# A fused S5 scan and gated MLP: the residual stored early and the gated product added to it by accumulating DMA, with a new order of the work

## The chip, the cores and the metric

The kernel runs on one core of one Trainium2 chip. Its engines, as the profile names them, are TensorE (PE, with its weight loads as PEld), VectorE (DVE), ScalarE (ACT), GpSimd (POOL) and SyncE (SP), which here only issues DMAs. The metric is device time of one execution in microseconds, as the median of several runs. A profiled execution also gives a trace: its span runs from the first to the last instruction and is a little shorter than the execution's time.

## The reference

The input `x` has 2048 tokens of 448 channels, in bfloat16. It is normalized twice: once as the input of both branches, and once more inside branch B.

```python
def _A_ref(x, Lambda_re, Lambda_im, B_re, B_im, C_re, C_im, log_dt, Dskip):
    dt = jnp.exp(log_dt)
    Lam_bar = jnp.exp(dt * Lam)
    B_bar = ((Lam_bar - 1.0) / Lam)[:, None] * Bmat
    Bu = jnp.einsum("bld,pd->blp", x + 0j, B_bar)
    for t in range(L):
        h = Lam_bar[None, :] * h + Bu[:, t, :]
    y = 2.0 * jnp.einsum("blp,dp->bld", hseq, Cmat).real + x * Dskip[None, None, :]

def _B_ref(x, w1, b1, w2, b2):
    y = _layernorm(x, axis=-1)
    h = _gelu(jnp.einsum("bsd,df->bsf", y, w1) + b1)
    return jnp.einsum("bsf,fd->bsd", h, w2) + b2

xn = _layernorm(x, axis=-1)
s = _A_ref(xn, A_Lambda_re, ...)
g = _silu(_B_ref(xn, B_w1, B_b1, B_w2, B_b2))
return x + s * g
```

Branch A is a complex diagonal recurrence over all 2048 tokens with 448 states. Branch B is an MLP with 1792 hidden units. The output is the residual `x` plus the product of both.

## The kernel before

The tokens are worked in four groups of 512. A group has two blocks (`b`), and a block two tiles of 128 tokens (`r`), so there are eight blocks and sixteen tiles. The 448 channels or states lie as three tiles of 128 and one of 64 on the partitions. For each group the kernel does the following.

- **Normalization.** `ln_stats` takes mean and variance of each tile of `x_all`: groups 0 and 1 on VectorE (BATCH_NORM_STATS2 and AGGREGATE, L441 and L445; L457 and L458 for the first group), groups 2 and 3 on ScalarE in two passes with an accumulator (L433 and L434, the groups in `SUMS`). `ln_scale` turns them into scales by a power on GpSimd or by two Newton steps on VectorE. `ln_apply` writes the normalized tiles `xn_sb` (for branch A) and `xn2_sb` (for branch B, both norms in one; the profile leaves numbers in names out and shows `xn_sb` for both), L514 on VectorE or L515 on ScalarE. `xt` transposes them by DMA into `xnT` and `xn2T`. The first group goes through `first_norm`: tile by tile, its scale by Ln and Exp on ScalarE or by a power on GpSimd (L462), and its transposes by TensorE, copied out of PSUM by L471 or L472.
- **Branch A.** `bu` multiplies `xnT` by the B matrices into `u_sb` (TensorE L665, and L685 for the last tile; copies out of PSUM at L682, L683, L687, L688). `ssm` rotates `u_sb` by cosine and sine tables (`WT`), so that a real scan with a decay is left (L709, seven scans of 512 tokens), and rotates the result back into `h_sb`. These rotations are the wide products of VectorE (L701 to L703 and L729 to L731, 128x3072). The end of a group's scan is turned into the start value `cur` of the next by four small GpSimd operations (L722 to L725), the carry.
- **Branch B.** `mm1` is the first layer of the MLP in seven pairs of hidden tiles (TensorE L665, Gelu on ScalarE L746). In the first group the pairs below `HALF` are done block by block, with matmuls of 256 columns (`mm1_half`, L758). `mm2` is the second layer (L779: 14 matmuls for each tile, 56 for a group), and Silu on ScalarE gives the gate `g_sb` (L782).
- **Output.** `ym` multiplies `h_sb` by the C matrices and `xnT` by the diagonal of `Dskip` (L796 and L799), VectorE multiplies by the gate into `t3` (L802, `t` in the profile), adds `x` for a whole block (L815, into `o_sb`, which the profile calls `tmp`), and SP stores it to `out`. The last block goes tile by tile, its last tile in two parts (L806).

The matmuls that keep TensorE busy before its first real work multiply `still` by itself (I0 to I9, L825).

All of this is written as tasks with what they read and write. The order is a table, `ORDER`, one list for all engines: each engine gets its tasks in that order and waits at each one for what the task depends on. `SECOND` says which tasks run on their second engine, and `BANKS` which of the eight PSUM banks each tile of results takes; a bank's next user waits until its last has been read. So an engine that waits holds up all that stands behind it on its queue. DMAs stand in the queue of the engine that issues them.

Of the kernel before, what the change touches and what calls it, by code (L numbers as in the profile page):

```python
# [10 lines left out]
F32 = dt.float32  # L11
# [36 lines left out]
class Plan:  # L48
# [50 lines left out]
    def dma(self, eng, out_ap, in_ap, reads=(), writes=(), prio=0.0, nbytes=0, transpose=False, dur=0.45):  # L99
        sem = f"d{self.ndma}"  # L100
        self.ndma += 1
        self._sem(sem)

        def fn(e):
            if transpose:
                return e.dma_start_transpose(out_ap, in_ap)
            return e.dma_start(out_ap, in_ap)  # L107
# [97 lines left out]
ST I2 11 I7 20 12 18 17 19 I1 75 76 0 1 13 16 15 2 3 14 80 81 22 23 I0 I3 21 5 9 I8 4 82 PV 77 24 25 27 36 26 78 6 7 T0 83 T2 I6 79 I4 I9 85  # L205
86 87 90 91 38 96 8 84 H010 92 88 34 93 H000 40 I5 T3 T1 95 144 41 46 97 89 101 118 94 42 43 45 10 H04 32 117 33 H001 39 98 102 109 115 110
H02 48 44 55 122 H011 105 116 223 119 49 56 47 103 106 H03 50 104 99 121 227 123 35 29 107 H05 28 100 H06 108 57 DH 51 54 53 61 111 311 222
224 228 124 125 112 120 138 225 128 229 193 113 312 129 126 58 64 313 114 59 60 62 65 66 67 226 206 207 198 194 230 231 232 31 30 145 238
202 314 127 130 235 69 199 131 132 135 203 137 233 208 209 133 136 234 396 200 195 204 241 196 166 240 315 205 201 397 197 U01 167 U00 U02
162 164 160 236 139 H13 242 134 237 163 141 63 165 317 316 239 169 H11 282 319 H10 68 283 161 170 320 168 318 171 172 173 174 180 398 H14  # L210
278 279 276 284 142 37 285 U10 H15 243 H12 181 70 74 286 280 179 176 277 52 143 177 175 U12 244 399 73 400 287 281 71 H16 247 72 183 288 178
140 248 289 146 148 149 147 150 151 182 189 321 H20 154 155 186 152 U11 187 361 290 153 184 245 246 323 156 158 185 291 293 188 295 402 362
401 403 249 157 190 191 192 297 159 405 218 254 253 219 404 294 216 406 325 322 298 210 292 250 212 296 326 217 255 211 H26 251 H35 H23 373
213 259 374 367 368 H21 454 327 252 261 363 324 262 263 258 260 455 U20 U22 H34 364 U21 328 265 256 257 329 330 332 452 220 H22 333 264 272
266 268 267 271 331 H24 273 274 275 339 338 340 453 365 369 370 269 H30 H33 444 450 307 308 214 445 270 334 343 411 299 305 300 366 335 410
451 221 345 301 H36 H25 412 H32 302 306 346 344 407 408 409 456 336 348 448 215 457 371 347 U30 U32 413 337 341 417 372 H31 449 342 418 414
349 U31 350 375 446 415 309 354 351 353 310 352 355 416 382 447 383 357 356 358 359 360 424 380 423 376 458 425 432 431 378 379 377 392 386
419 459 420 429 384 428 433 421 430 435 393 422 426 465 427 303 434 440 381 436 463 437 460 304 439 441 438 442 443 387 385 461 390 467 388
389 391 394 462 464 469 395 468 473 470 471 472 477 474 475 476 466 478 479 480 481 482 483 484
""".split()]  # L220
SECOND = [int(k) if k.isdigit() else k for k in """
77 79 84 87 94 115 130 150 161 167 183 187 230 270 316 317 319 320 322 323 325 326 355 407 408 410 411 418
""".split()]
BANKS = [int(k) if k.isdigit() else k for k in """
3 3 0 0 1 5 1 3 3 2 5 3 0 6 5 0 4 2 2 0 6 6 0 2 0 2 4 5 6 7 4 5 4 6 1 2 6 0 4 0 4 2 0 6 0 2 6 6 4 7 5 6 1 0 1 2 6 0 7 2 6 2 2 0 6 0 2 3 4 5
3 2 6 1 0 0 2 3 6 6 4 4 4 4 2 6 0 5 7 4 5 6 5 4
# [12 lines left out]
def bass_recurrent_scan__ssm_conv_s5__mixer_channel_mlp__prompt_kernel(  # L239
# [14 lines left out]
    NB, NG, NF, NK, HALF = 8, 4, 14, 512, 2  # L254
    PK, SUMS = 3, (2, 3)
# [3 lines left out]
    with ExitStack() as es:  # L259
# [6 lines left out]
        eps = SB("eps", [128, 1], F32)  # L266
# [24 lines left out]
        junk = SB("junk", [128, D])  # L291
# [19 lines left out]
        t3 = SB("t3", [128, 2, 2, D])  # L311
# [24 lines left out]
        with nc.Block():  # L336
# [13 lines left out]
            preload("natural_log_exp_and_others", [], "logs", "exp")  # L350
            pool(lambda e: e.memset(eps[:], LN_EPS * LN_EPS), [], ["eps"], 0.1)
# [75 lines left out]
            def ln_stats(g, blocks=(0, 1)):  # L427
                if g in SUMS:
                    for b in blocks:
                        for r in range(2):  # L430
                            q = r * 2 + b
                            src, mv = x_all[:, xa(2 * g + b, r), :], lnmv[:, g % 2, q, :]
                            act([lambda e, src=src, mv=mv: e.activation(junk[:], src, ACT.Identity, scale=-1.0 / D, accum_out=mv[:, 0:1]),  # L433
                                 lambda e, src=src, mv=mv: e.activation(junk[:], src, ACT.Square, bias=mv[:, 0:1], accum_out=mv[:, 1:2])],  # L434
                                [f"x{2 * g + b}"], [f"mv{g % 2}_{q}", "junk"], 1.3)
                            kb.tasks[-1].chain = True
                    return
# [44 lines left out]
            def ln_scale(g, blocks=(0, 1)):  # L482
# [14 lines left out]
                if sign < 0:  # L497
                    power.append(lambda e: e.tensor_scalar(w(3), w(3), -1.0, None, op0=ALU.mult))
# [399 lines left out]
```

## Time and profile before

| | |
|---|---|
| time, median of three runs | 149.23 us (149.13 to 149.49) |
| profiled execution | 149.4 us |
| its span | 147.7 us |
| TensorE busy | 141.8 us, 96% |
| VectorE busy | 128.1 us, 87% |
| ScalarE busy | 106.3 us, 72% |
| GpSimd busy | 46.0 us, 31% |
| granted TensorE clock | 1.000 |

Busy time is an average over a start, a long full middle and a tail, and these have different limits. So the chain of work that ended last, and the waits of the engines on it, say more than the shares. A row of a group gives the line, the engine, the operation, output and inputs, shapes and count; then the busy time, the mean of one in ns, and the idle time before them with what ended it. In a timeline row the first two numbers are start and length in us.

### The profile page before, as it was taken

Reading aid. Unit: us, or ns where it says so; the run is one execution under the profiler, and the core shown is the slowest. Engines: PE = TensorE matmul, PEld = TensorE weight load, DVE = VectorE, ACT = ScalarE, POOL = GpSimd, SP = SyncE. Lnnn points to the kernel's source line nnn. Section 1 sums busy time; section 2 is a strip of 40 time slices with the busy share of each in tenths; the row PEclk is TensorE's granted clock in tenths of the full one; section 3 lists DMA queues with packets and bytes.
Section 4 is the critical chain, followed back from the end, with each engine's and each line's share of the span. In section 5 each row is a group of like instructions: output and inputs, shape, how many; then the busy total and the mean of one; then the engine's idle time right before and its main releaser. Section 6 shows DMA issues by size and latency. Waiting matters only on the chain.

```text
span 147.7 us, 2854 instructions
## 1 busy us (share of the span) xinstructions
PE 141.8 (96%) x1078; PEld 74.6 (51%) x1078; DVE 128.1 (87%) x168; ACT 106.3 (72%) x173; POOL 46.0 (31%) x89
## 2 busy tenths in 40 slices
PE   6979999998999999999998999999999999999992
PEld 2557744543555545555553454555435455555562
DVE  1846999806599999999999998999999999999994
ACT  2469899899999999999939997962999112291300
POOL 2488788930009592800000003900009300000000
DMA  4989999998859101007080002019003000103033
GB/s 103 286 249 388 274 307 150 198 95 157 158 127 96 28 18 22 0 0 142 18 157 8 0 18 80 4 22 204 16 7 98 0 0 0 40 0 98 0 127 124
DMA packets 32084, 14.09 MB, mean 95 GB/s; under 512 B 24131, under 2 KB 31686, under 8 KB 32070
## 3 DMA queue, kind: packets, MB, share of 16 engines
q1 hardware_dynamic: 31376, 13.83, 42.7%
q8 instruction: 8, 0.13, 0.4%
q10 hardware_dynamic: 694, 0.07, 0.4%
q14 instruction: 6, 0.05, 0.1%
HBM read 5.63 MB, written 1.84 MB: 51 GB/s over the span
## 4 chain that ended last, share of the span: by engine, by line
PE 86%; DMA 6%; DVE 4%; SPq 2%; issue 1%; ACT 0%; ACTq 0%; DVEq 0%
PE psum L665 37%; PE psum L779 29%; PE psum L796 14%; DMA xnT<-xn_sb 3%; DMA x_all<-in_A_x_dram 3%; PE psum L685 2%; PE psum L799 2%; SPq L107 2%; DVE t L802 1%; PE psum L771 1%; DVE lnst L457 1%; DVE xn_sb L514 1%; DVE WT L621 0%; PE psum L469 0%; DVE tmp L806 0%
## 5 line engine op out<-in xcount | busy, mean ns | idle before, releaser
L665 PE MATMUL psum<-xn2T,w_sb 64*128 64x512 bf16 (+1 forms) x420 | 45.2, 362 | 0.9 <-ACT cw L547 0.9
L779 PE MATMUL psum<-w_sb,gT 128*128 128x448 bf16 x224 | 43.7, 353 | 0.1
L746 ACT ACTIVATE gT<-psum,b1f 128x512 bf16<-128x512 f32 x52 | 32.1, 688 | 8.0 <-PE psum L665 7.8
L665 PEld LDWEIGHTS psum<-xn2T,w_sb 64*128 64x128 bf16 x420 | 24.4, 108 | 18.9 <-ACT cw L547 1.0
L779 PEld LDWEIGHTS psum<-w_sb,gT 128*128 128x128 bf16 x224 | 21.5, 98 | 21.6 <-issue 1.5
L709 DVE TENSOR_TENSOR_SCAN s_f<-cw,cur,v_sb 128x512 f32<-128x512 f32 x21 | 25.5, 1266 | 0.0
L796 PE MATMUL psum<-CQ,h_sb 128*128 128x448 bf16 (+2 forms) x119 | 24.8, 342 | 0.0
L665 PE MATMUL psum<-xnT,BT 64*128 64x512 bf16 x168 | 20.4, 376 | 1.0 <-DVE xn_sb L514 0.6
L722 POOL TENSOR_TENSOR cwk<-s_f,ang 128x8 f32<-128x8 f32 x3 | 3.5, 1166 | 45.5 <-ACT s_f L719 45.5
L782 ACT ACTIVATE g_sb<-psum 128x448 bf16<-128x448 f32 x16 | 8.1, 536 | 10.7 <-PE psum L779 10.6
L796 PEld LDWEIGHTS psum<-CQ,h_sb 128*128 128x128 bf16 x119 | 10.9, 98 | 7.5 <-issue 0.4
L665 PEld LDWEIGHTS psum<-xnT,BT 64*128 64x128 bf16 x168 | 8.3, 94 | 11.0 <-PE psum L665 1.2
L713 ACT ACTIVATE s_b<-s_f 128x3072 bf16<-128x3072 f32 x4 | 11.1, 2774 | 2.9 <-DVE s_f L709 2.8
L682 ACT ACTIVATE u_sb<-psum 128x1024 bf16<-128x1024 f32 x10 | 10.1, 1019 | 0.4 <-PE psum L665 0.3
L515 ACT ACTIVATE xn_sb<-x_all,lnw 128x512 bf16<-128x512 bf16 x13 | 10.1, 810 | 0.0
L802 DVE TENSOR_TENSOR t<-psum,g_sb 128x448 bf16<-128x448 f32 (+2 forms) x17 | 9.7, 587 | 0.3 <-PE psum L796 0.2
L709 DVE TENSOR_TENSOR_SCAN s_f<-cw,v_sb 128x512 f32<-128x512 f32 x7 | 8.1, 1208 | 0.0
L601 POOL TENSOR_TENSOR DG<-ident,Dbc 128x128 bf16<-128x128 bf16 (+1 forms) x4 | 3.6, 917 | 13.3 <-DMA Dbc<-in_A_Dskip_dram 13.3
L825 PE MATMUL psum<-still 128*128 128x128 bf16 (+1 forms) x30 | 6.4, 364 | 1.2 <-DVE still L339 1.0
L730 DVE TENSOR_TENSOR pb<-s_b,WT 128x3072 bf16<-128x3072 bf16 x4 | 7.0, 1752 | 0.4 <-ACT s_b L713 0.3
L703 DVE TENSOR_TENSOR v_sb<-pa,pb 128x3072 bf16<-128x3072 bf16 x4 | 7.0, 1756 | 0.1
L731 DVE TENSOR_TENSOR h_sb<-pa,pb 128x3072 bf16<-128x3072 bf16 x4 | 7.0, 1755 | 0.1
(123 smaller groups left out, 175.2 us busy)
## 6 DMA issues: line engine op xcount, KB each, us to landing
out_dram<-tmp SPq DMA_DIRECT2D x7, 224.0 KB, 2.3
w_sb<-in_B_w_dram SPq DMA_DIRECT2D x6, 256.0 KB, 5.2
x_all<-in_A_x_dram SPq DMA_DIRECT2D x3, 448.0 KB, 6.8
w_sb<-in_B_w_dram SPq DMA_DIRECT2D x3, 448.0 KB, 7.5
u_sb<-u_sb SPq DMA_DIRECT2D x8, 64.0 KB, 2.1
s_b<-s_b SPq DMA_DIRECT2D x8, 64.0 KB, 1.9
w_sb<-in_B_w_dram SPq DMA_DIRECT2D x2, 128.0 KB, 3.1
x_all<-in_A_x_dram SPq DMA_DIRECT2D x2, 112.0 KB, 2.5
```

The source lines that it names most:

```text
L515: ("act", lambda e: e.activation(dst, src, ACT.Identity, bias=nb, scale=rs), 0.81)]
L665: return lambda e: e.matmul(out(k), wt(k, d, halves[h]), rhs(k, d, halves[h]), start=first and d == 0, stop=not first and d == 3)
L682: kb.either(("act", lambda e: e.activation(u_sb[:, i, :, :], psum[:, bank.b:bank.b + 2, :], ACT.Copy), 1.02), ("dve", lambda e: e.tensor_c ...
L703: dve(lambda e: e.tensor_tensor(v_sb[:, 0:3, :, :], pa[:], pb[:], ALU.add), ["pa", "pb"], ["v"], 1.76)
L709: dve(lambda e, i=i, ri=ri, init=init: e.tensor_tensor_scan(s_f[:, i, ri, :], col(R1, i).to_broadcast([128, NK]), v_sb[:, i, ri, :], init, ...
L713: act(lambda e: e.activation(s_b[:, 0:3, :, :], s_f[:, 0:3, :, :], ACT.Copy), SF, ["sb"], 2.76)
L730: dve(lambda e: e.tensor_tensor(pb[:], wide(s_b, 1), WT[:, 0:3, 1:3, :], ALU.mult), ["sb"] + WK, ["pb"], 1.76)
L746: act([lambda e, k=k: e.activation(gT[:, gb, 2 * j + k, :], psum[:, bank.b + k, :], ACT.Gelu_apprx_tanh, bias=b1f[:, 2 * j + k:2 * j + k + ...
L779: fns = [lambda e, fi=fi, bk=bk, q=q: e.matmul(psum[:, bk.b, 0:D], gT[:, gb, fi, q * 128:(q + 1) * 128], w2_sb[:, fi, :], start=False, sto ...
L782: act(lambda e, gs=gs, bk=bk: e.activation(g_sb[:, gs, :], psum[:, bk.b, 0:D], ACT.Silu), [bk.key] + (["silu"] if g == 0 else []), [f"g{gs ...
L796: fns = [lambda e, k=k: e.matmul(psum[:, bank.b, c0:c1], h_sb[:, hb, k, k0:k0 + 128], CQ[:, k, c0:c1], start=(k == 0), stop=(k == 6)) for ...
L802: dve(lambda e: e.tensor_tensor(t3[:, ob, r, c0:c1], psum[:, bank.b, c0:c1], g_sb[:, gs, c0:c1], ALU.mult), [bank.key, f"g{gs}"], [f"t3{ob ...
```

## The change

- Seven of the eight blocks of `x` are stored to `out` by SP as soon as they are loaded. Where VectorE added `x` to a block's gated product and SP stored the sum (L815), GpSimd now issues a DMA that adds `t3` to what lies in `out`. It waits for the block's two gate multiplies and for the early store. `t3` has four buffers instead of two. The last block is done as before.
- The statistics of all groups are taken on VectorE; `SUMS` and the ScalarE passes are gone.
- The first group's scales all come from a power on GpSimd; the multiply and add before it stands on VectorE. Ln and Exp, their table and `eps` are gone, and ScalarE loads the Gelu table at once.
- `HALF` is 3 instead of 2: one more pair of hidden tiles of the first group is done block by block.
- `ORDER`, `SECOND` and `BANKS` are new. Among what moves: the first block's second load of `x` (`x1`) stands ahead of the first weights on SP, one 128x2048 Abs of the tables goes to ScalarE, five normalizations go from VectorE to ScalarE, and on GpSimd the first of the accumulating DMAs stands between the first and the second carry, the next between the second and the third, and five behind the third.

```diff
@@ dma
+            if accum:
+                return e.dma_start(out_ap, in_ap, accum_op=ALU.add)
@@ tables of the order
-ST I2 11 I7 20 12 18 17 19 I1 75 76 0 1 13 16 15 2 3 14 80 81 22 23 I0 I3 21 5 9 I8 4 82 PV 77 24 25 27 36 26 78 6 7 T0 83 T2 I6 79 I4 I9 85
+ST I0 11 17 12 13 18 I3 9 16 4 20 0 I1 14 15 22 21 19 24 23 I7 10 I2 1 74 75 79 80 76 77 84 81 82 T0 85 86 89 I5 T2 90 8 I6 I8 87 91 78 I4
...
-    NB, NG, NF, NK, HALF = 8, 4, 14, 512, 2
-    PK, SUMS = 3, (2, 3)
+    NB, NG, NF, NK, HALF = 8, 4, 14, 512, 3
+    PK = 3
-        t3 = SB("t3", [128, 2, 2, D])
+        t3 = SB("t3", [128, 4, 2, D])
-            preload("natural_log_exp_and_others", [], "logs", "exp")
+            preload("gelu_apprx_tanh_and_others", [], "warm", "gelu")
@@ ln_stats
-                if g in SUMS:
-                    for b in blocks:
...
-                            act([lambda e, src=src, mv=mv: e.activation(junk[:], src, ACT.Identity, scale=-1.0 / D, accum_out=mv[:, 0:1]),
-                                 lambda e, src=src, mv=mv: e.activation(junk[:], src, ACT.Square, bias=mv[:, 0:1], accum_out=mv[:, 1:2])],
...
@@ first_norm
-                        dve(lambda e, q=q: e.bn_aggr(lnmv[:, 0, q, :], lnst[:, q, :]), [f"st{q}"], [f"mv0_{q}"], 0.18)
-                        t = kb.either(("act", [lambda e, var=var, r1=r1: e.activation(r1, var, ACT.Ln, scale=1.0 + LN_EPS, bias=eps[:]),
-                                               lambda e, r1=r1: e.activation(r1, r1, ACT.Exp, scale=-0.5)], 0.53),
...
+                        kb.add("dve", [lambda e, q=q: e.bn_aggr(lnmv[:, 0, q, :], lnst[:, q, :]),
+                                       lambda e, var=var, w0=w0: e.tensor_scalar(w0, var, 1.0 + LN_EPS, LN_EPS * LN_EPS, op0=ALU.mult, op1=ALU.add)],
+                               [f"st{q}"], [f"mv0_{q}", f"w0{q}"], dur=0.3, chain=True)
+                        pool(lambda e, w0=w0, r1=r1: e.tensor_tensor(r1, w0, mhalf[:, 0, :], ALU.pow), [f"w0{q}", "mhalf"], [f"r1{q}"], 0.57)
...
@@ ym
-                gs, ob = n % 8, b
+                gs, ob = n % 8, (2 * g + b) % 4
...
                 if r and not last:
-                    t = xa(2 * g + b, 0)
-                    o2r = o_sb[:, ob, :].rearrange("p (r d) -> p r d", r=2)
-                    dve(lambda e: e.tensor_tensor(o2r, t3[:, ob, :, :], x_all[:, t:t + 3:2, :], ALU.add), [f"t3{ob}_0_0", f"t3{ob}_1_0"] + xk(2 * g + b),
-                        [f"o{ob}_0_0", f"o{ob}_1_0", f"o{ob}_1_256"], 0.64)
-                    kb.dma("sp", dram_ap(out, off, [[D, 128], [256 * D, 2], [1, D]]), o2r,
-                           reads=[f"o{ob}_0_0", f"o{ob}_1_0", f"o{ob}_1_256"], writes=[f"out{g}{b}"], nbytes=229376)
+                    kb.dma("pool", dram_ap(out, off, [[D, 128], [256 * D, 2], [1, D]]), t3[:, ob, :, :],
+                           reads=[f"t3{ob}_0_0", f"t3{ob}_1_0", f"out{g}{b}"], writes=[f"sum{g}{b}"], nbytes=229376, dur=1.2, accum=True)
@@ main
+            for k in range(2 * NG - 1):
+                t = xa(k, 0)
+                kb.dma("sp", dram_ap(out, xrow(k), [[D, 128], [256 * D, 2], [1, D]]), x_all[:, t:t + 3:2, :],
+                       reads=xk(k), writes=[f"out{k // 2}{k % 2}"], nbytes=229376)
```

The tables move instructions on every engine. Three places show it, with the lines of the kernel that the rows belong to (the changed kernel's line numbers are 11 to 18 lower). The first is VectorE at the start, in `first_norm`. Before:

```order
L457 BN_STATS lnst<-x_all 128x6
L458 BN_AGGR lnmv<-lnst 128x2
L457 BN_STATS lnst<-x_all 128x6
L458 BN_AGGR lnmv<-lnst 128x2
L465 TENSOR_SCALAR xn_sb<-x_all,lnmv,lnw 128x512 x2
L457 BN_STATS lnst<-x_all 128x6
L458 BN_AGGR lnmv<-lnst 128x2
L457 BN_STATS lnst<-x_all 128x6
```

With the change, where L448 is the small scale before the power:

```order
L446 BN_STATS lnst<-x_all 128x6
L447 BN_AGGR lnmv<-lnst 128x2
L448 TENSOR_SCALAR lnw<-lnmv 128x1
L446 BN_STATS lnst<-x_all 128x6
L447 BN_AGGR lnmv<-lnst 128x2
L448 TENSOR_SCALAR lnw<-lnmv 128x1
L451 TENSOR_SCALAR xn_sb<-x_all,lnmv,lnw 128x512
L446 BN_STATS lnst<-x_all 128x6
L451 TENSOR_SCALAR xn_sb<-x_all,lnmv,lnw 128x512
```

Each tile has one instruction more, and the third tile's statistics stand between the normalizations of the first two. The second place is ScalarE between the first group's last Gelu and the first copies of `u_sb`. Before:

```order
L348 ACT_TABLE_LOAD
L619 ACTIVATE WT<-s_f 128x4x512
L782 ACTIVATE g_sb<-psum 128x448
L620 ACTIVATE WT<-s_f,sgn 128x4x512
L433 ACTIVATE junk,lnmv<-x_all 128x448
L434 ACTIVATE junk,lnmv<-x_all,lnmv 128x448
L782 ACTIVATE g_sb<-psum 128x448 x2
L433 ACTIVATE junk,lnmv<-x_all 128x448
L434 ACTIVATE junk,lnmv<-x_all,lnmv 128x448
L782 ACTIVATE g_sb<-psum 128x448
L682 ACTIVATE u_sb<-psum 128x1024 x2
```

With the change:

```order
L498 ACTIVATE xn_sb<-x_all,lnw 128x512 x2
L553 ACTIVATE ang<-ang 128x16
L348 ACT_TABLE_LOAD
L602 ACTIVATE WT<-s_f 128x4x512
L598 ACTIVATE s_f<-s_f 128x4x512
L603 ACTIVATE WT<-s_f,sgn 128x4x512
L498 ACTIVATE xn_sb<-x_all,lnw 128x512 x2
L765 ACTIVATE g_sb<-psum 128x448 x3
L498 ACTIVATE xn_sb<-x_all,lnw 128x512
L665 ACTIVATE u_sb<-psum 128x1024 x2
L765 ACTIVATE g_sb<-psum 128x448
L665 ACTIVATE u_sb<-psum 128x1024
```

The statistics are gone, an Abs over the table (L598) and normalizations (L498) have come, and no Silu stands between the two Sin. The third place is TensorE behind the first group's output tiles. Before (L665 with `xnT` is `bu`, with `xn2T` it is `mm1`):

```order
L799 MATMUL psum<-DG,xnT 128x128
L796 MATMUL psum<-CQ,h_sb 128x448 x6
L665 MATMUL psum<-xn2T,w_sb 128x512 x56
L665 MATMUL psum<-xnT,BT 128x512 x16
L665 MATMUL psum<-xn2T,w_sb 128x512 x8
L665 MATMUL psum<-xnT,BT 128x512 x26
```

With the change (L762 is `mm2`):

```order
L782 MATMUL psum<-DG,xnT 128x128
L779 MATMUL psum<-CQ,h_sb 128x448 x6
L762 MATMUL psum<-w_sb,gT 128x448 x28
L668 MATMUL psum<-xnT,BT 128x512 x4
L648 MATMUL psum<-xnT,BT 128x512 x36
```

Half of the second group's `mm2` has come behind the output tiles, and the third group's `mm1` pairs that stood there now stand ahead of them.

More of the change, by code (lines that the diff above doesn't have):

```diff
@@ L209 @@
[L209 to L216, printed above, removed]
@@ L479, in first_norm @@
                                 lambda e: e.tensor_tensor(n0, mean, r0, ALU.mult), lambda e: e.tensor_scalar(n0, n0, -1.0, None, op0=ALU.mult)],
-                       [f"mv0_{q}" for q in range(4)] + ["mhalf"], ["lnw0_0", "lnw0_1"], dur=1.2, chain=True)
+                       [f"mv0_{q}" for q in range(4)] + ["mhalf"], ["lnw0_0", "lnw0_1"], dur=1.6, chain=True)
             def ln_scale(g, blocks=(0, 1)):
```

56 lines of the change are left out of this document (24 added, 32 removed).

## The prediction

> **What bounds the kernel now.** I read the page first: the busy times, then the chain that ended last.
>
> ```profile
> span 147.7 us, 2854 instructions
> PE 141.8 (96%) x1078; PEld 74.6 (51%) x1078; DVE 128.1 (87%) x168; ACT 106.3 (72%) x173; POOL 46.0 (31%) x89
> PE 86%; DMA 6%; DVE 4%; SPq 2%; issue 1%; ACT 0%; ACTq 0%; DVEq 0%
> ```
>
> TensorE is busy in 96% of the span and makes 86% of the chain. The change takes none of its real work away, so time can come only from before its first real matmul, from its holes, and from what follows its last one. The second view is busy time by stage (columns: stretch, its length, busy us of PE, PEld, DVE, ACT, POOL, granted clock, DMA share, GB/s).
>
> ```profile
> 40.00:80.00 40.00, 39.57 (x308) 20.56 (x304) 39.31 (x40) 37.11 (x59) 12.92 (x14) 1.00 0.35 60
> 80.00:120.00 40.00, 40.00 (x316) 19.62 (x313) 38.68 (x37) 29.54 (x41) 10.54 (x8) 1.00 0.17 41
> 120.00:140.00 20.00, 20.00 (x122) 10.77 (x120) 19.70 (x20) 7.25 (x10) 0.00 (x0) 1.00 0.10 25
> ```
>
> From 40 us on VectorE is as full as TensorE (39.31 and 38.68 of 40), and until 80 ScalarE nearly so (37.11). The clock is 1.00 throughout. Three engines are close to setting the end at once, so relief of one is worth little unless the others follow. Third, the chain in order of time (start, us, what):
>
> ```profile
> 8.88 1.07 PE psum L665 x16
> 10.96 9.35 PE psum L665 x104
> 21.37 1.26 PE psum L779 x6
> 22.68 9.63 PE psum L779 x50
> 35.56 18.95 PE psum L665 x174
> 75.08 4.68 DMA xnT<-xn_sb
> ```
>
> And the waits of TensorE behind its holes (us in total, times, longest):
>
> ```profile
> PE psum L665 <- DVE xn_sb L514: 0.6, 1, 0.6
> PE psum L665 <- DMA xnT<-xn_sb: 0.4, 1, 0.4
> ```
>
> Real matmuls start at 8.88, run on without a pause from 10.96, and have holes of 0.6 (before 35.56) and 0.4 (at 79.8, behind the transpose begun at 75.08). Last, the end, by the timeline:
>
> ```profile
> 138.06 0.43 DVE L733 TENSOR_TENSOR h_sb<-pa 128x512 bf16<-128x512 bf16 x1
> 138.91 0.36 PE L799 MATMUL psum<-DG,xnT 128*128 128x128 bf16 x4
> 144.33 0.66 PE L796 MATMUL psum<-CQ,h_sb 128*128 128x192 bf16 x6
> 145.50 0.26 DVE L806 TENSOR_TENSOR tmp<-t,x_all 128x192 bf16<-128x192 bf16 x1
> ```
>
> TensorE ends at 144.33+0.66 = 144.99, and 2.7 us follow (gate, add, last store). The last group's four output tiles need `h_sb`, which VectorE finishes at 138.49; the first of them begins about 0.2 before its diagonal matmuls of 138.91. So VectorE leads by only some 0.2 us there.
>
> **The change part by part.** The sum is made against the profiled execution: 149.4 us, the span of 147.7 and 1.7 around it. It lies 0.17 above the median of the three runs, 149.23.
>
> ```profile
> L815 DVE TENSOR_TENSOR tmp<-t,x_all 128x896 bf16<-128x896 bf16 x7 | 4.3, 618 | 0.3 <-DMA out_dram<-tmp 0.2
> L441 DVE BATCH_NORM_STATS2 lnst<-x_all 128x6 f32<-128x448 bf16 x4 | 2.4, 617 | 0.0
> L445 DVE BATCH_NORM_AGGREGATE lnmv<-lnst 128x2 f32<-128x6 f32 x4 | 0.7, 168 | 0.0
> L683 DVE CAST u_sb<-psum 128x1024 bf16<-128x1024 f32 x2 | 2.5, 1225 | 2.8 <-PE psum L665 2.8
> L434 ACT ACTIVATE junk<-x_all,lnmv 128x448 bf16<-128x448 bf16 x8 | 5.3, 668 | 0.3
> ```
>
> *VectorE.* The residual adds go: 7 x 0.618 = 4.3 us. The statistics of groups 2 and 3 come from ScalarE, 8 x 0.617 + 8 x 0.168 = 6.3; all eight BATCH_NORM_STATS2 lie ahead of the first wide product, beside TensorE's first group, where VectorE has room. In the full stage, from the first wide product (39.83 before) to the last group's `h_sb`, I count: 4 adds fewer (-2.5; the other three stood behind `h_sb`), one gate multiply moved behind it (-0.6), 4 aggregates (+0.7), one CAST of `u_sb` more (+1.2), and one scaling of `tmp`, one small cast and one DG tile (+1.0, estimated from operations of that size). That is -0.2 of some 98 us: in this stage the relief is spent again. The last `h_sb` then follows the first wide product, which waits for ScalarE (holes, below), and comes at 137.5 to 138.7; TensorE will want it at about 138.1. I charge 0.1, bounds 0 and 0.6.
>
> *ScalarE* loses the two passes per tile of its statistics (the second alone is 5.3 us) and gains five normalizations and an Abs over 2048 columns; the gain is cover in the stage where it is nearly full.
>
> *Start.* `x1` is loaded ahead of the first weights; all first scales come from POOL; VectorE has one more small instruction per tile and takes the second tile's statistics before it normalizes the first.
>
> ```profile
> 3.40 0.63 DVE L457 BATCH_NORM_STATS2 lnst<-x_all 128x6 f32<-128x448 bf16 x1 [2.41 <-DMA x_all<-in_A_x_dram]
> 4.67 0.56 POOL L462 TENSOR_TENSOR lnw<-lnw,mhalf 128x1 f32<-128x1 f32 x1
> 6.72 1.09 ACT L472 ACTIVATE xn2T<-psum 128x512 bf16<-128x512 bf16 x2 [1.13 <-PE psum L469]
> 8.48 0.16 ACT L547 ACTIVATE cw<-psum 128x12 f32<-128x12 f32 x1
> ```
>
> From 3.40 two tiles of statistics, aggregate and small scale (about 1.0 each, the power of 0.56 beside them), the first normalization, the third tile's statistics and the second normalization end at about 6.95. Transposes and the second ScalarE copy (half of 1.09) end at 8.0. Before, 8.88 was set by the parameter copy that ends at 8.64; now that copy stands behind. So the first real matmul comes at 8.0, and the fourth tile's transposes end at about 9.75 (before: 10.96). In between only 8 matmuls of 256 columns fit (before: 16 by 9.95). What is left behind 9.75 is 76 half and 56 full matmuls: HALF 3 splits one more pair. A full one is 18.95/174 = 0.109, a half one 1.07/16 = 0.067: 5.1+6.1 = 11.2 with 0.3 for the bias; by the same prices 70 full and 40 half were 10.6 before, measured 10.41. The first group ends at 9.75+11.3 = 21.1 instead of 21.37: -0.2, bounds -0.6 and +0.4.
>
> *Old holes.* The 0.6 was a wait for a normalization on VectorE; it is replaced by the bank waits below (-0.6). At the 0.4, two of group 1's four output tiles of the MLP (28 matmuls, 28 x (1.26+9.63)/56 = 5.4 us) now stand between the tile that frees `xnT` and the matmuls that read it; the transpose takes 4.7. So -0.4, with 0.7 us of cover; without that cover the full 4.7 would show.
>
> *New holes.* At 20 to 40 us ScalarE does what VectorE did, and TensorE's next banks wait for it.
>
> ```profile
> L348 ACT ACT_TABLE_LOAD x3 | 3.8, 1283 | 2.9 <-issue 2.8
> L619 ACT ACTIVATE WT<-s_f 128x2048 bf16<-128x2048 f32 x1 | 1.9, 1910 | 0.4 <-ACT L348 0.4
> L515 ACT ACTIVATE xn_sb<-x_all,lnw 128x512 bf16<-128x512 bf16 x13 | 10.1, 810 | 0.0
> L682 ACT ACTIVATE u_sb<-psum 128x1024 bf16<-128x1024 f32 x10 | 10.1, 1019 | 0.4 <-PE psum L665 0.3
> L782 ACT ACTIVATE g_sb<-psum 128x448 bf16<-128x448 f32 x16 | 8.1, 536 | 10.7 <-PE psum L779 10.6
> ```
>
> A run of Gelu from the timeline shows how such operations follow each other:
>
> ```profile
> 49.33 2.40 ACT L746 ACTIVATE gT<-psum,b1f 128x512 bf16<-128x512 f32 x4
> ```
>
> From 21.1: two Gelu pairs (2.3), two normalizations (1.6), a small Abs, the table load and the 0.4 behind it (1.9), three operations over 2048 columns (5.8), two normalizations (1.6), three Silu (1.6): 14.8, which frees the bank of the third `bu` tile at 35.9; a normalization, two copies, a Silu and a copy more (4.3) bring the third `u_sb`, and with it VectorE's first wide product, to 40.2. Operations in a row overlap (four Gelu in 2.40, where four times the single one is 2.75), so 34.9 and 39.0 are as likely. TensorE reaches the third `bu` tile at 21.1 + 10.9 (MLP) + 28 x 0.109 = 35.1, and the next group's first bank, freed by the second copy, at 37.6, against 37.6 to 38.6. Holes here: 0 to 1.0. From 55 to 70 the Gelu pairs again free TensorE's banks at about the time that it wants them: 0 to 0.4 more. I take 0.5, nearer the overlapped end.
>
> *Stores and accumulating DMAs.* Seven stores of `x` leave the SP queue between the transposes of the first two groups and later.
>
> ```profile
> 88.27 0.52 SPq L107 DMA_DIRECT2D out_dram<-tmp  x1
> ```
>
> Each holds the transposes behind it up by one such issue (0.52). At the first group the transposes leave at about 24 and 26 and are wanted at 32.0, when the MLP ends: 4.7 to landing leaves over 1 us, so 0; with that cover gone each store costs its 0.5. The tail's last add and store stay as they are.
>
> Sum: -0.2 - 0.6 - 0.4 + 0.5 + 0.1 = -0.6, so 148.8 against the profiled execution, and **148.6** against the median.
>
> **The rivals.** *The last accumulating DMA ends last* (slower). It starts when the gate multiply before the last block is done, 2.4 us before TensorE ends (two tiles of 1.5 less 0.6). Before shows no DMA issued by POOL and none that adds.
>
> ```profile
> out_dram<-tmp SPq DMA_DIRECT2D x7, 224.0 KB, 2.3
> x_all<-in_A_x_dram SPq DMA_DIRECT2D x1, 224.0 KB, 3.7
> ```
>
> To landing it is bounded by a store (2.3) and a load and a store one after the other (6.0). For POOL's own part, three of the carry's operations:
>
> ```profile
> 59.10 0.48 POOL L722 TENSOR_TENSOR cwk<-s_f,ang 128x8 f32<-128x8 f32 x1 [2.97 <-ACT s_f L719]
> 90.87 1.77 POOL L722 TENSOR_TENSOR cwk<-s_f,ang 128x8 f32<-128x8 f32 x1 [28.43 <-ACT s_f L719]
> 96.18 0.20 POOL L725 TENSOR_TENSOR cur<-cwk 128x4 f32<-128x4 f32 x1
> ```
>
> Its issue I bound by a short and a long one (0.5 and 1.8). It decides from 2.4+2.7 = 5.1 us on. The middle, 1.2+3.5 (nearer the store, since both directions can overlap), is hidden by 0.4; the long end, 7.8, costs 2.7, and a typical bad case (1.2+6.0) 2.1: 150.7. For it: three of these DMAs leave within the last 7 us. Against it: the store part alone lands in 2.3. By the Trainium skill ("DMA: Bandwidth & Descriptors", Anatomy of one DMA) a DMA from GpSimd takes about 2.0 us plus bytes over 436 GB/s; an estimate by that is 2.5 us for this one, which would be hidden; no run here shows it yet.
>
> *POOL is held up while it issues* (slower). The same 8-column product took 0.48 at 59.10 and 1.77 at 90.87, when VectorE ran its wide products; the first accumulating DMA stands ahead of the second carry on POOL. Counted from the start of ScalarE's long `s_b` copy, ScalarE gives the carry its input after some 6 us, the carry's four products take 5.5 (90.87 to 96.38, the last with its 0.20), and VectorE asks for it after some 14.5 (a scan, a cast, two gate multiplies and seven wide products with their small ones). So 3 us are to spare, and the DMA costs nothing until its issue takes 9; one that is held through the whole run of wide products, 11.6 us, would cost 3: 151.6. The Trainium skill speaks against such a DMA ("SBUF — State Buffer", the "DVE blocks DMA" trap): GpSimd cannot write descriptors while VectorE holds the shared port. Its section Who interferes with whom takes plain tensor_tensor out of that, and by it the cost is 0; the rows above show the hold for compute on POOL only.
>
> *The holes move and nothing is won* (no change). ScalarE comes at the late end (holes 1.4 instead of 0.5) or a transpose is late once: 149.0 to 149.6. For it: each cover above is below 1 us, and ScalarE was 37.11 of 40 full.
>
> *More is won*: no new hole and a start at its bound: 147.7 to 147.9.
>
> **How the numbers follow.** Forecast (147.9 to 148.8) 0.45, more 0.05, no change 0.26, last DMA 0.16, POOL held up 0.08. A run of this kernel tells about 0.3% (0.45 us) from no change, so "faster" is below 148.78. Faster 0.5; same 0.26; slower 0.24. The likeliest case's own range is 147.9 to 149.0; for 8 in 10 it runs from 147.7 to 150.5, which takes in the typical bad end of the DMA's unknown landing in part.
>
> **What would show it.** Right: the first real matmul near 8.0 and the first group's end near 21.1; no wait of TensorE for `xnT` at the third group; TensorE's end near 144.4; VectorE's last `h_sb` ahead of it; the last accumulating DMA landing before the last store. Wrong: waits of TensorE for ScalarE at 35 to 38 above 1 us; VectorE's scans waiting for `cur` behind POOL; an accumulating DMA that lands more than 5 us after its gate multiply and ends the chain.

## The result: 1.3% slower

The changed kernel takes 150.86 us (median; 150.76 to 151.08), the kernel before in the same comparison 149.18. The ratio is 1.0127, with a 95% interval of 1.0086 to 1.0167. The forecast was 148.6 with a range up to 150.5, so sign and range are both wrong; what came is close to the 150.7 that had been worked out for the first rival, partly by luck, as is shown at the end. Three executions fell into a slow state and are left out of all times and ratios below: two with all seven accumulating DMAs in the kernel before (153.55 and 154.16) and one of the kernel before (379.37).

The page of the changed kernel: span, busy times, and the shares of the chain that ended last.

```profile
span 148.8 us, 2865 instructions
PE 142.4 (96%) x1092; PEld 74.0 (50%) x1092; DVE 125.3 (84%) x176; ACT 98.8 (66%) x144; POOL 48.3 (32%) x96
PE 41%; DVE 20%; ACT 2%; issue 1%; DVEq 0%
```

The chain starts from VectorE's last operation. The profile follows it back to 50.6 us, so its shares do not add up to 100%. From 107.2 until the last `h_sb` at 138.4 it runs almost wholly over VectorE, where in the kernel before TensorE makes 86% of it. The DMAs behind VectorE's last operation are not in it.

The profiled execution took 150.88, so 2.08 lie outside the span; in the kernel before it was 149.4-147.7 = 1.7. Inside, the timeline (start, us, engine and line) answers the rows shown before.

```profile
7.95 0.61 PE L648 MATMUL psum<-xn2T,w_sb 64*128 64x256 bf16 x8
20.16 11.47 PE L762 MATMUL psum<-w_sb,gT 128*128 128x448 bf16 x56
31.57 4.06 PE L648 MATMUL psum<-xnT,BT 64*128 64x512 bf16 x36
137.99 0.43 DVE L716 TENSOR_TENSOR h_sb<-pa 128x512 bf16<-128x512 bf16 x1
144.09 0.66 PE L779 MATMUL psum<-CQ,h_sb 128*128 128x192 bf16 x6
145.26 0.26 DVE L789 TENSOR_TENSOR tmp<-t,x_all 128x192 bf16<-128x192 bf16 x1
```

TensorE ends at 144.75, 0.24 ahead of the kernel before (144.99), and VectorE at 145.52 instead of 145.76. So up to the last operation of an engine the change is a little faster than the profiled execution of before. Behind it, the span runs on for 148.8-145.52 = 3.28 us, where the kernel before needed 147.7-145.76 = 1.94. What fills that time is told by four views. First the DMA that lands last, the store of 48 KB behind VectorE's last operation (KB, then us to landing, counted from the start of the issue). Before:

```profile
out_dram<-tmp SPq DMA_DIRECT2D x1, 48.0 KB, 1.5
```

With the change:

```profile
out_dram<-tmp SPq DMA_DIRECT2D x1, 48.0 KB, 2.9
```

Second, a wait in SP's list at the end of the changed kernel (us in total, times, longest):

```profile
SPq L196 <- DMA out_dram<-t: 1.7, 1, 1.7
```

Then GpSimd's timeline at the end:

```profile
139.78 2.42 POOL L108 DMA_DIRECT2D out_dram<-t  x2 [21.71 <-DVE t L785]
142.98 1.19 POOL L108 DMA_DIRECT2D out_dram<-t  x1 [0.77 <-DVE t L785]
```

And busy time by stage, with the columns that the prediction names; the last two are the share of the 16 DMA engines and GB/s:

```profile
141.00:144.00 3.00, 3.00 (x25) 2.01 (x24) 1.42 (x4) 0.00 (x0) 2.23 (x2) 1.00 0.97 104
144.00:147.00 3.00, 0.97 (x14) 0.80 (x12) 1.45 (x5) 0.00 (x0) 0.17 (x1) 1.00 1.08 157
```

The same stages of the kernel before:

```profile
141.00:144.00 3.00, 3.00 (x24) 1.93 (x23) 2.70 (x5) 0.00 (x0) 0.00 (x0) 1.00 0.46 153
144.00:147.00 3.00, 0.99 (x13) 0.74 (x10) 1.66 (x6) 0.00 (x0) 0.00 (x0) 1.00 0.48 153
```

At its end SP asks for one DMA after the other. It waits 1.7 us for the last accumulating one, which lands 5.2 us from the start of its issue, at 148.2. The last store, issued at 145.6, lands later still, at 148.5, and the span ends at 148.8. So what ends the kernel is this store, and its 1.4 us more to landing are the longer tail. From 141 to 147 the DMA engines are full (0.97 and 1.08 of 16 engines), and yet they move about what they moved before at less than half the share: 104 and 157 GB/s against 153 and 153. Three accumulating DMAs are issued there, two from 139.78 on and the last from 142.98.

### The profile page after: what moved, and what is told of

Its sections match the earlier page's. It is cut to its first block, busy times and chain, and to the rows that moved or that the text cites. A ratio compares the mean times of both kernels' runs of the same rounds, so it can differ in the third digit from the quotient of the medians.

```text
span 148.8 us, 2865 instructions
## 1 busy us (share of the span) xinstructions
PE 142.4 (96%) x1092; PEld 74.0 (50%) x1092; DVE 125.3 (84%) x176; ACT 98.8 (66%) x144; POOL 48.3 (32%) x96
## 3 DMA queue, kind: packets, MB, share of 16 engines
q0 software_dynamic: 1904, 1.61, 9.2%
## 4 chain that ended last, share of the span: by engine, by line
PE 41%; DVE 20%; ACT 2%; issue 1%; DVEq 0%
PE psum L648 21%; PE psum L779 10%; PE psum L762 7%; DVE s_f L692 6%; DVE h_sb L714 2%; DVE pa L712 2%; DVE pb L713 2%; ACT s_b L696 2%; PE psum L782 1%; PE psum L668 1%; DVE v_sb L686 1%; DVE pa L684 1%; DVE pb L685 1%; DVE pa L715 1%; DVE t L785 1%
## 5 line engine op out<-in xcount | busy, mean ns | idle before, releaser
L762 PE MATMUL psum<-w_sb,gT 128*128 128x448 bf16 x224 | 44.2, 353 | 0.2
L729 ACT ACTIVATE gT<-psum,b1f 128x512 bf16<-128x512 f32 x50 | 30.4, 704 | 6.5 <-PE psum L648 6.5
L762 PEld LDWEIGHTS psum<-w_sb,gT 128*128 128x128 bf16 x224 | 21.3, 98 | 22.2 <-PE psum L762 1.5
L692 DVE TENSOR_TENSOR_SCAN s_f<-cw,cur,v_sb 128x512 f32<-128x512 f32 x21 | 26.0, 1271 | 0.1
L108 POOL DMA_DIRECT2D out_dram<-t x7 | 8.7, 1323 | 37.1 <-DVE t L785 37.0
L498 ACT ACTIVATE xn_sb<-x_all,lnw 128x512 bf16<-128x512 bf16 x18 | 14.1, 811 | 0.2
L430 DVE BATCH_NORM_STATS2 lnst<-x_all 128x6 f32<-128x448 bf16 x12 | 6.9, 607 | 7.3 <-DMA x_all<-in_A_x_dram 7.3
L665 ACT ACTIVATE u_sb<-psum 128x1024 bf16<-128x1024 f32 x10 | 10.1, 1027 | 0.9 <-PE psum L648 0.8
L705 POOL TENSOR_TENSOR cwk<-s_f,ang 128x8 f32<-128x8 f32 x3 | 1.6, 527 | 27.0 <-ACT s_f L702 23.0
L685 DVE TENSOR_TENSOR pb<-u_sb,WT 128x3072 bf16<-128x3072 bf16 x4 | 7.0, 1754 | 3.1 <-ACT u_sb L665 3.1
L712 DVE TENSOR_TENSOR pa<-s_b,WT 128x3072 bf16<-128x3072 bf16 x4 | 7.0, 1749 | 0.8 <-ACT s_b L696 0.8
L684 DVE TENSOR_TENSOR pa<-u_sb,WT 128x3072 bf16<-128x3072 bf16 x4 | 7.2, 1811 | 0.1
```

The source lines that it names most:

```text
L108: return e.dma_start(out_ap, in_ap, accum_op=ALU.add)
L498: ("act", lambda e: e.activation(dst, src, ACT.Identity, bias=nb, scale=rs), 0.81)]
L665: kb.either(("act", lambda e: e.activation(u_sb[:, i, :, :], psum[:, bank.b:bank.b + 2, :], ACT.Copy), 1.02), ("dve", lambda e: e.tensor_c ...
L684: dve(lambda e: e.tensor_tensor(pa[:], wide(u_sb, 0), WT[:, 0:3, 1:3, :], ALU.mult), U + WK, ["pa"], 1.76)
L692: dve(lambda e, i=i, ri=ri, init=init: e.tensor_tensor_scan(s_f[:, i, ri, :], col(R1, i).to_broadcast([128, NK]), v_sb[:, i, ri, :], init, ...
L712: dve(lambda e: e.tensor_tensor(pa[:], wide(s_b, 0), WT[:, 0:3, 0:2, :], ALU.mult), ["sb"] + WK, ["pa"], 1.76)
```

## The experiments

The theory after the first profile, called A, was that these late DMAs are the loss; the rival B, that the new order as such is slower. All times are medians of a comparison with the kernel before on the same chip, where no single execution is named; "tail" is the span behind VectorE's last operation in the profiled execution.

### Late blocks the old way, and the write without the adding

The first kernel lets blocks 4, 5 and 6 go the old way in the changed kernel:

```diff
-                if r and not last:
+                if r and 2 * g + b in (4, 5, 6):
+                    dve(lambda e: e.tensor_tensor(o2r, t3[:, ob, :, :], x_all[:, t:t + 3:2, :], ALU.add), ...)
+                    kb.dma("sp", dram_ap(out, off, ...), o2r, ...)
+                elif r and not last:
                     kb.dma("pool", dram_ap(out, off, ...), t3[:, ob, :, :], ..., accum=True)
```

> The changed kernel, but blocks 4, 5 and 6 (the three whose accumulating DMAs leave after 139 us) go the old way: no early store of x for them, VectorE adds x (0.62 us each), SP stores. Blocks 0 to 3 still accumulate. Theory A (the three late accumulating DMAs keep the DMA engines busy from 141 to 148 and so the last stores land late): the last store lands some 1.9 us behind VectorE's last operation again, as in the kernel before, instead of 3.3; span 147.3 to 147.8, time 149.2 to 149.8. If the extra 0.35 us outside the span (150.88-148.8 against 149.4-147.7) belongs to any DMA issued by GpSimd, it stays: the upper half of that range. Theory B (the new order as such is slower, whatever the way of the output): 150.5 or more, with TensorE's end later than 144.75.

Measured: 149.18 us (149.10 to 149.51), ratio to before 1.0028 (1.0009 to 1.0047). So 1.68 us are gone with three DMAs. What is left of the loss, 0.5 us above the 148.66 of the kernel before in this comparison, is not theirs. VectorE's last operation in this kernel's timeline:

```profile
144.89 0.26 DVE L790 TENSOR_TENSOR tmp<-t,x_all 128x192 bf16<-128x192 bf16 x1
```

And its last stages:

```profile
141.00:144.00 3.00, 3.00 (x29) 2.19 (x28) 2.86 (x7) 0.00 (x0) 0.00 (x0) 1.00 0.45 154
144.00:147.00 3.00, 0.57 (x9) 0.40 (x6) 1.07 (x4) 0.00 (x0) 0.00 (x0) 1.00 0.45 143
```

The span is 147.1, so the tail is 147.1-145.15 = 1.95 again, and the DMA engines are less than half full.

The second keeps all seven DMAs on GpSimd, but they overwrite instead of adding:

```diff
-                return e.dma_start(out_ap, in_ap, accum_op=ALU.add)
+                return e.dma_start(out_ap, in_ap)
```

> The changed kernel, with the seven DMAs of GpSimd writing their block instead of adding to it; so the residual x is left out of seven of the eight blocks. Theory A1 (it is the adding that makes the DMA engines slow: 224 KB keep them busy longer than a plain store): the three late DMAs land in about 2.5 us instead of 4.2 to 5.4, the last store is no longer held up, span 147.4 to 147.8, time 149.4 to 149.9. Theory A2 (it is GpSimd's queue, whatever the DMA does): landing, span and time as in the changed kernel, 150.6 to 151.0.

Measured: 149.43 us, ratio 1.0039 (1.0023 to 1.0056); tail 147.4-145.46 = 1.94. So it is the adding (A1), not GpSimd's queue. The DMA parts of both pages show its price (queue: packets, MB, share of 16 engines over the span; then the issues: KB each, us to landing). The changed kernel:

```profile
q0 software_dynamic: 1904, 1.61, 9.2%
out_dram<-t POOLq DMA_DIRECT2D x7, 224.0 KB, 4.5
```

The kernel that overwrites:

```profile
q0 software_dynamic: 560, 1.61, 3.2%
out_dram<-t POOLq DMA_DIRECT2D x7, 224.0 KB, 2.5
```

The bytes that the profile counts are the same, but an accumulating DMA of 224 KB is cut into 1904/7 = 272 packets instead of 80. That is about one for each output row of 896 bytes, of which a block has 256. In time it is 0.092 x 148.8 / 7 = 1.96 us of all 16 engines, against 0.032 x 147.4 / 7 = 0.67. Three of them are 5.9 us of work. It starts at about 141.5, so by this sum it lasts until about 147.4; the stores of the last block, issued from 144.33 to 145.6, share the engines with it.

### Which of the three

> The changed kernel, but block 6 alone goes the old way (no early store of x, an add of 0.62 us on VectorE, a store by SP); blocks 4 and 5 still accumulate, from 139.8 and 141.0. Theory Q (each accumulating DMA keeps all 16 DMA engines busy for about 2 us; only work queued behind them counts): the two are through by 145.5, the last stores, issued at 144.3 to 145.6, hardly wait: span 147.2 to 147.7, time 149.2 to 149.7. Theory L (the long landing of the last accumulating DMA ends the kernel, the others don't matter): the last of them lands by 146.5, ahead of the last store: 149.2, as with all three of them gone.

> The changed kernel, but blocks 4 and 5 go the old way; block 6 accumulates, from about 143.0. Theory Q: with nothing queued ahead of it this one has the DMA engines from 144.3 to 146.4 and shares them with the last block's stores, which land some 0.5 to 1.0 late: span 147.5 to 148.2, time 149.6 to 150.2. Theory L: its landing takes 4.2 to 5.4 from the issue whatever is ahead: it lands at 147.2 to 148.4, time 149.3 to 150.5; a time of 150.5 or more speaks for L, and a landing that got shorter with the two others gone for Q.

The edit is the one above with `(6,)` and with `(4, 5)`. With blocks 4 and 5 accumulating: 149.25 us, ratio 1.0031 (1.0007 to 1.0056), tail 1.94; they cost nothing. With block 6 alone: 150.36, ratio 1.0101 (1.0064 to 1.0139), a little above the range given by theory Q and inside that of theory L. Its timeline:

```profile
141.34 1.15 DVE L786 TENSOR_TENSOR t<-psum,g_sb 128x448 bf16<-128x448 f32 x2
143.03 1.19 POOL L108 DMA_DIRECT2D out_dram<-t  x1 [24.52 <-DVE t L786]
145.19 0.26 DVE L790 TENSOR_TENSOR tmp<-t,x_all 128x192 bf16<-128x192 bf16 x1
```

SP's waits for the accumulating DMA and then for the stores, and the last store:

```profile
SPq L196 <- DMA out_dram<-t: 0.8, 1, 0.8
SPq L196 <- DMA out_dram<-tmp: 0.5, 2, 0.3
out_dram<-tmp SPq DMA_DIRECT2D x1, 48.0 KB, 2.3
```

The span ends at 148.2, a tail of 2.75. The gate multiply ends at 142.49 and the issue starts 0.54 later. Counted from that start, the DMA lands after 4.1 us, at 147.1, with nothing queued ahead of it: 4.6 behind the multiply. With the two others ahead it took 5.2, so by the sign set above, a landing that got shorter, this speaks for theory Q. Theory L fails: SP still waits for stores after the accumulating DMA has landed. The last store, issued at 145.5, takes 2.3 us to landing instead of 1.5, which is the 0.8 of longer tail; with the two DMAs ahead it takes 2.9. So an accumulating DMA costs here by what it takes from the stores beside and behind it.

### The DMAs in the kernel before

Here blocks 0 to 6 of the kernel before get the new output way, with four buffers of `t3`; in the order, the early stores stand behind the transposes at 45 us and each accumulating DMA where its add stood:

```diff
                 if r and not last:
-                    dve(lambda e: e.tensor_tensor(o2r, t3[:, ob, :, :], x_all[:, t:t + 3:2, :], ALU.add), ...)
-                    kb.dma("sp", dram_ap(out, off, ...), o2r, ...)
+                    kb.dma("pool", dram_ap(out, off, ...), t3[:, ob, :, :], ..., accum=True)
...
+            for k in range(2 * NG - 1):
+                kb.dma("sp", dram_ap(out, xrow(k), ...), x_all[:, t:t + 3:2, :], ...)
```

> The kernel before with the output way of the change alone: early stores of x for blocks 0 to 6 on SP (one after the other, behind the transposes at 45 us), no adds on VectorE for these blocks, seven accumulating DMAs on GpSimd at the places of the adds, four buffers of t3. Order, start and statistics as before. Theory A: VectorE loses 2.5 us ahead of the last h_sb, but TensorE, which sets the end, gains at most 0.3 there; the late accumulating DMAs make the tail 3.3 instead of 2.0 and the time outside the span 2.05: 150.3 to 151.2. Theory B (the loss is in the new order): 148.7 to 149.4, the same as before.

Measured: 151.1 us, ratio 1.0144 (1.0101 to 1.0188), in theory A's range of time. But only 1.0 of it is the tail (149.3-146.34 = 2.96). The rest came from a place that I had not named. In the waits of TensorE stands:

```profile
PE psum L667 <- DMA xnT<-xn_sb: 1.5, 1, 1.5
```

And in GpSimd's timeline:

```profile
71.08 1.45 POOL L108 DMA_DIRECT2D out_dram<-t  x1 [9.11 <-DVE t L804]
73.97 1.20 POOL L108 DMA_DIRECT2D out_dram<-t  x1 [1.44 <-DVE t L804]
```

Two accumulating DMAs start just ahead of the transposes of `xnT` (72.62 and 75.09), and TensorE's wait for these went from 0.4 (none in the second profile below) to 1.5. An accumulating DMA thus also costs in the middle, if something that is waited for is queued behind it. Two kernels separate the two places. The first does this for the late three only (`4 <= 2 * g + b < 7` in that condition):

> The kernel before with the new output way for its last three blocks but one only (4, 5 and 6): early stores of x behind the transposes at 45 us, no adds on VectorE for these three, and three accumulating DMAs where the adds stood, the last of them some 2.4 us ahead of TensorE's end. Everything else, blocks 0 to 3 too, as before. Theory Q (about 2 us of all DMA engines for each, and the last block's stores behind them): the span's tail behind VectorE's last operation goes from 2.0 to 3.2 or 3.3, VectorE's part before the last h_sb is unchanged: 149.8 to 150.4 where before is 148.7, that is 1.1 to 1.7 more. Theory B (the loss is the new order's, not the DMAs'): 148.4 to 149.0.

Measured: 150.10 us, ratio 1.0085 (1.0054 to 1.0117), in theory Q's range; VectorE's last operation ends at 144.94 and the span at 148.3, a tail of 3.36. The second does it for blocks 0 to 3 (`2 * g + b < 4`), with the four DMAs behind GpSimd's third carry, where no transpose is near:

> The kernel before, with the new output way for blocks 0 to 3 only: early stores of x behind the transposes at 45 us, no adds on VectorE for these four, and the four accumulating DMAs one after the other on GpSimd behind its third carry, at about 116 to 121, where no transpose and no store is queued. Theory Q (an accumulating DMA costs only by the 2 us of DMA engines that it keeps from work queued behind it): no cost here; VectorE loses 2.5 us ahead of its last h_sb and TensorE's wait for it (0.1 to 0.2) goes: 0 to 0.4 faster than before, which is 148.7 to 148.9 in the last two comparisons. Theory C (accumulating DMAs cost wherever they stand, by a fixed amount for their queue): 0.3 or more slower than before.

Measured: 148.58, ratio 0.9998 (0.9974 to 1.0023). No cost, as theory Q says, but no gain either: with 2.5 us less for VectorE ahead of it, TensorE's weight loads still wait for the last `h_sb`. The timeline has both, the four issues and that wait:

```profile
114.68 5.17 POOL L108 DMA_DIRECT2D out_dram<-t  x4
137.54 0.10 PEld L798 LDWEIGHTS psum<-CQ,h_sb 128*128 128x128 bf16 x1 [0.38 <-DVE h_sb L735]
```

Part of the 2.5 us went into VectorE's own waits. From 39.8 to 137.5 it is idle for 3.8 us here, against 2.3 and 2.0 in two traces of the kernel before; the waits for ScalarE's copy `s_b` are 1.4 in all instead of 0.3 and 0.5, and one for the DMA of `u_sb` is 0.6 instead of none and 0.3. Where the rest went is not traced.

### The new order without the DMAs

The edit of the first experiment, with all seven blocks in its list and no early store left:

```diff
-                if r and 2 * g + b in (4, 5, 6):
+                if r and 2 * g + b in range(7):
```

> The changed kernel with no accumulating DMA and no early store of x at all: seven adds on VectorE and seven stores by SP, at the places in the order where the accumulating DMAs stood. The new order, the new start and the new statistics stay. Theory A (the DMAs cost, the order gains little): VectorE has 4 adds (2.5 us) more before the last group's h_sb, of which it has little room; TensorE ends 0 to 2.0 later than 144.75, but the tail is 2.0 again and the time outside the span 1.7: 148.8 to 150.8. Theory B (the new order as such is slower): 151 or more. If the time outside the span returns to 1.7, the 0.35 is the price of having DMAs of GpSimd's queue at all.

Measured: 156.24, far outside. The trace shows a fault of the edit and not of the theory: the store of block 1 stood on SP ahead of two transposes and waited for its add (at 102.50), and TensorE behind them for 3.9 us (from 100 to 120 the granted clock was 0.91, elsewhere 1.00):

```profile
108.78 5.38 PE L649 MATMUL psum<-xnT,BT 64*128 64x512 bf16 x36 [3.90 <-issue]
```

With the stores of blocks 0 to 3 moved in the order, behind the transposes and the wrapped columns:

> The changed kernel without any accumulating DMA or early store of x, as in the run before with seven adds on VectorE, but the stores of blocks 0 to 3 stand on SP behind the transposes and the wrapped columns that they held up there by 3.9 us. So this is the new order, start and statistics alone. VectorE has 2.5 us more to do before the last h_sb than in the changed kernel, and that chain was the critical one there from 107 us on: TensorE ends 0 to 2.5 later than 144.4 (its end with the last three blocks the old way), the tail is 2.0 and 2.05 lies outside the span: 149.2 to 151.7, most likely 150.5. If it comes out at 149.2 or less, VectorE had room for the adds and the accumulating DMAs brought nothing even off the tail.

Measured: 150.59, ratio 1.0116 (1.0069 to 1.0163), tail 1.88. TensorE waits for the last `h_sb`:

```profile
PE psum L780 <- DVE h_sb L717: 0.8, 1, 0.8
```

So the new order, which moves statistics to VectorE, needs the relief: accumulating blocks 0 to 3 is worth 150.59-149.18 = 1.4 us there, and nothing in the order before. Theory B was right in part: by itself the new order is slower, 150.59 against 148.86. Blocks 0 to 3 win back 1.4, and blocks 4 to 6 then lose 1.7 at the end of the kernel. In no comparison is the new order faster than the kernel before: the best medians are 149.18 and 149.25.

### A second profile of the kernel before

No edit:

> The kernel before, unchanged, for a second profile: its runs fall into two groups, 148.3 to 148.6 and 149.1 to 149.5, and the profile that the prediction was made from is of the upper one. Expected: either group. If the lower one, its trace should show at which of the holes (0.6 before 35.56, 0.4 at 79.8) or in which stretch the 0.8 us lie.

This execution took 147.59, below both groups. Its timeline:

```profile
7.76 1.07 PE L665 MATMUL psum<-xn2T,w_sb 64*128 64x256 bf16 x16
20.27 11.00 PE L779 MATMUL psum<-w_sb,gT 128*128 128x448 bf16 x56
34.13 2.98 PE L665 MATMUL psum<-xnT,BT 64*128 64x512 bf16 x26 [0.16 <-ACT g_sb L782]
77.79 1.89 PE L665 MATMUL psum<-xnT,BT 64*128 64x512 bf16 x16
143.69 0.26 DVE L806 TENSOR_TENSOR tmp<-t,x_all 128x192 bf16<-128x192 bf16 x1
```

The first real matmul comes at 7.76 instead of 8.88, the hole of 0.6 is 0.16, that of 0.4 is gone. It is a single execution, the fastest on record. Single runs of the kernel before lie between 147.6 and 149.8, with medians of 148.66, 148.86, 148.66 and 149.02 in the four later comparisons; the execution that the prediction was made from, 149.4, was near the upper end.

### The time outside the span

Runs with the order before spend 1.67 to 1.81 us outside the span, also with accumulating DMAs; runs with the new order 2.00 to 2.14, also without any. Two variants of the kernel of the first experiment, run once each, tried to find the cause: an unused first table load on ScalarE, and the last four idle matmuls moved to the start.

```diff
+            preload("natural_log_exp_and_others", [], "logs", "exp")
             preload("gelu_apprx_tanh_and_others", [], "warm", "gelu")
```

> The changed kernel with its last three blocks the old way (149.18 us, of which 147.1 span and 2.05 outside), plus one table load of ScalarE that nobody uses: that of the natural logarithm and exponential, as the first one, ahead of the Gelu table, where ScalarE idles until 5.9. All kernels with the old order showed 1.69 to 1.78 outside the span and all with the new one 2.00 to 2.14, with and without accumulating DMAs. If the first table that a program loads decides that, the time outside falls to 1.75 and the span stays at 147.0 to 147.6: 148.8 to 149.3. If not: 2.05 outside.

And in the order:

```diff
-ST I0 11 17 ...
-... I9 ...
+ST I0 I9 11 17 ...
```

> The same kernel (last three blocks the old way), with TensorE's last four idle matmuls, which the new order runs behind its last real one, moved back to the start. If they at the end make the time outside the span, it falls from 2.05 to 1.75; if not, it stays. The span stays at 147.0 to 147.6.

Both took 149.30 us: 147.4 in the span and 1.9 outside with the table load, and 147.3 and 2.0 with the idle matmuls moved. The idle matmuls are not it. For the table the one value lies between both bands and settles nothing. What makes these 0.3 us stays open.

## Why the prediction was wrong, step by step

- **The stores and accumulating DMAs, costed at 0: this step failed.** The sentence that failed is "The tail's last add and store stay as they are". The last store took 2.9 us to landing instead of 1.5, because three accumulating DMAs, 5.9 us of engine time, were still at work; that is the 1.34 of longer tail. The rival priced one DMA alone, although its text said that three leave in the last 7 us. For one alone its middle price was right: 4.7 forecast from the multiply to the landing, 4.6 measured with block 6 alone, and the issue took 1.19 (forecast 1.2). But that hidden DMA still cost 0.8, since it held up the stores beside it, a cost for which neither the sum nor a rival had a term. With three the last one landed 5.7 behind its multiply, over the rival's 5.1, and still ahead of the last store. So the sign "the last accumulating DMA landing before the last store" came true and did not mean that the DMAs were hidden. The rival named the right DMAs, but not how they cost, and its 150.7 against the measured 150.86 is partly luck: it added 2.1 to a gain of 0.6 that did not come, where the tail lost 1.34 and the rest of the kernel lost instead of gaining. The estimate of 2.5 us from the Trainium skill ("DMA: Bandwidth & Descriptors", Anatomy of one DMA) agrees with the DMA that overwrites (2.5 to 2.7), not with the one that adds (4.2 to 5.4 in the changed kernel).
- **Baseline and old holes (-0.6 and -0.4): right in the trace, wrong in the sum.** Both are gone in the changed kernel, but the second profile shows them nearly gone in the unchanged one too. Waits that one execution shows were priced as if each had them.
- **Start, -0.2.** The first real matmul was right (8.0, measured 7.95). The first group ended at 20.16 instead of 21.1: the last transposes were 0.3 sooner, and 132 matmuls took 10.73 instead of 11.3. (The prices written there give 5.1+6.1+0.3 = 11.5; 11.3 was carried on.) By its price of 0.109 for a full matmul, the row of 76 half and 50 full ones (9.73) leaves 0.056 for a half one, where 0.067 was taken. But 0.6 of that is lost in the MLP of this group, 31.57-20.16 = 11.41 against 32.14-21.31 = 10.83, which I had not foreseen and did not trace further; and the second profile of before reaches the same point at 20.27. Against that one the start gains 0.1.
- **New holes, +0.5 (bounds 0 to 1.4).** Measured 0.8, within the bounds, at another place: none at 35 to 38, but at 43 and 50, in the waits of TensorE

```profile
PE psum L648 <- ACT gT L729: 0.6, 1, 0.6
PE psum L668 <- ACT u_sb L665: 0.2, 1, 0.2
```

- **The last `h_sb`, +0.1.** Forecast 137.5 to 138.7, measured 138.42. TensorE lost 0.24 to it (a run of 1.73 instead of 1.49), within the bounds of 0 to 0.6.
- **TensorE's end.** Forecast 144.4, measured 144.75, by start, holes and `h_sb` together.
- **GpSimd held up while it issues: did not happen.** All seven issues take 1.19 to 1.66 us in the changed kernel. At 115.66, with VectorE busy for 0.90 to 1.00 of each microsecond, two take 2.42; no scan waits for `cur`. The trap that the prediction cited from the Trainium skill ("SBUF — State Buffer", "DVE blocks DMA") is told there of VectorE's two-port operations; beside these two issues VectorE ran tensor_tensor alone, so they do not test it. The Trainium skill's section Who interferes with whom on that page, which lets plain tensor_tensor out, agrees with these issues.

So the 2.2 us against a typical run of before (148.7) are 1.34 of tail, 0.3 outside the span (open) and 0.5 inside: such a run has its last operation at about 148.7-1.74-1.94 = 145.0, the changed kernel at 145.52. The 0.5 inside is not explained either: the same kernel with blocks 4 to 6 the old way has its last operation at 145.15.

## What to carry to other kernels

An accumulating DMA is not a store with a free add: price it by its packets and its engine time, here three times that of a plain write, and also by what it takes from the DMAs beside it, even when its own landing is hidden. Place it where nothing that is waited for is queued behind it, and not among the last stores. Work taken off an engine is worth only what that engine's chain makes others wait, 1.4 us in one order and nothing in the other. And a wait that a single trace shows is not a wait of each run: profile the baseline more than once before summing tenths.

## What the hardware showed that I had not expected

- An accumulating DMA of 224 KB goes as 272 packets and takes 1.96 us of all 16 DMA engines; the same DMA without the adding as 80 packets and 0.67 us. In these two kernels its issue on GpSimd takes 1.19 to 1.66 instead of 0.73 to 0.99.
- Four of them in a row: the timeline row above has 5.17 us for their issues, and each lands 4.6 to 6.6 us from the start of its issue.
- The same program's first matmul may come at 7.76 or at 8.88, and its time at 147.6 to 149.8, at a clock of 1.00.
